# Linear attention and a noisy top-2 mixture of experts: where row buffers lie, which scatters go first, and when the first expert's weights are loaded

## The chip, the cores and the metric

The kernel runs on one core of a Trainium2 chip. The metric is the device time of one execution in microseconds (us). The engines are TensorE (PE; PEld is its weight load), VectorE (DVE), ScalarE (ACT), GpSimd (POOL) and SyncE (SP), which only issues DMAs here.

## The reference

```python
def _attn_ref(q, k, v, lam):                 # q, k, v: 4 x 8 x 768 x 64
    ...
    for b in range(nb):                      # blocks of 64 positions
        intra = np.einsum('bhic,bhjc->bhij', qb, kb) * Dmask[None]
        intra = np.einsum('bhij,bhjd->bhid', intra, vb)
        inter = np.einsum('bhid,bhde->bhie', qb * lam_pow[None], kv_state)
        out[:, :, sl] = intra + inter
        kb_dec = kb * rev_pow[None]
        kv_state = lam_block[None, :, None, None] * kv_state + np.einsum('bhsd,bhse->bhde', kb_dec, vb)
    return out
...
x = attn_out.transpose(0, 2, 1, 3).reshape(B * S, H * D)      # 3072 tokens of 512
...
def _moe_ref(x, w_gate, w_noise, noise, w1, w2):              # 8 experts, 512 -> 1024 -> 512
    noisy_logits = x @ w_gate + np.log1p(np.exp(x @ w_noise)) * noise
    top2 = np.argpartition(-noisy_logits, 2, axis=1)[:, :2]
    ...                                      # softmax over the two chosen logits: top2_w
    for e in range(E):
        for k in range(2):
            mask = top2[:, k] == e
            h = np.maximum(x[mask] @ w1[e], 0.0)
            out[mask] += top2_w[mask, k, None] * (h @ w2[e])
    return out
```

## The kernel before

The order of the instructions on every engine is written out by hand (a manual schedule): each engine runs its instructions in program order, and semaphores are put where data or memory asks for them.

**Attention.** Twelve steps (`for t in range(NST)`, L911) work on two chunks of 128 positions each. A step turns the previous step's output into token rows: `products` and `turn_x` (L424) make transposes on PE, ACT copies them into a row buffer `xc` (two buffers), and `store_x` sends the rows to `x_tok` in DRAM. It transposes keys and queries of the next step (`trans_k`, `trans_q`), updates the state (`kv`), and makes this step's output (`intra`, `inter`, `evac_o`). SP's one queue takes, in program order, the loads of q, k and v three steps ahead, the row stores, the weight loads (`LOADS`) and the zero fill of the output (`zero_out`).

**Expert 0's weights** are loaded in eight pieces of 128 x 1024 floats (512 KB) into `wst` (four buffers, which also hold the one-hot tables `hot` of the routing). Each is split into a high part, a copy on ACT (`HIGH`, `split_high`), and a low part, a subtraction on POOL (`LOW`, `split_low`, L771), in the step that the dictionaries at L61 to L63 name. The last two pieces are split within the expert layers.

**Routing** runs in three groups of eight chunks. `routing(b)` is a generator of small DVE instructions, of which `advance(n)` issues the next n between other work. At its end each group has 16 scatters to send (one for each chunk and choice): indirect DMAs issued by POOL that write records (token, weight) into the list `lst` in DRAM. `scatter(n)` issues the next n; `paced(n, tile)` first puts a small POOL copy of the tile ahead, so that POOL doesn't run ahead of it. `finish(b, False)` issues what is left of a group's DVE instructions.

**From attention to experts.** When the attention pools `ac` and `aw` are closed (L973), the pool `hp` is laid over the same memory, beginning with `ht`, the first layer's output, 128 x 8 x 1664 floats, and then rows of 512 floats: `pv0`, `pv1`, `xg2`, `pv2`, up to `pv6`. An instruction that writes one of the new tiles first waits for everyone who used an old tile under it; for a new tile it waits at its first write, for all old tiles that any part of it covers. Within a pool a name gets its place when it is first used, in the order of first uses, with all its buffers side by side. `xc` is first used at L178 for a constant `hsel`, `kd` in `kdecay(0)` (L337).

Expert 0 takes its tokens in three parts of 2, 2 and 3 tiles of up to 128 tokens (`PARTS0`), gathered from `x_tok` by index (`gather_rows`), transposed and split (`trans_rows`, L818 to L821), through the first layer (`mm1`, L834; `evac1`, L840 on ACT and L844 on DVE) and the second (`gemm2`, L872). Record lists are loaded by SP (`load_rec`). Lists of expert 1 and the gathers of its rows come at L1008 to L1015, in the last part of expert 0: they need all 48 scatters. Then experts 1 to 7 follow in an order by size.

Of the kernel before, what the change touches and what calls it, by code (L numbers as in the profile page):

```python
# [21 lines left out]
FT = mybir.dt.float32  # L22
# [8 lines left out]
B, H, S, D = 4, 8, 768, 64  # L31
C = 128
NC = S // C
NCH = B * NC
HP = H // 2
DM = H * D
DB = DM // 128
# [17 lines left out]
NST = NCH // 2  # L55
# [2 lines left out]
MAXT = 24  # L58
FILLA, FILLB, FILLC = {4: 24, 5: 24, 6: 20, 7: 20, 8: 19, 9: 19, NST - 1: 24}, 2, 4
FILL1, FILL2 = 4, 9  # L60
LOADS = {3: [(1, 0)], 5: [(1, 1)], 6: [(1, 2)], 7: [(1, 3)], 8: [(2, 0)], 9: [(2, 1)], 11: [(2, 2), (2, 3)]}  # L61
HIGH = {5: [(1, 0)], 6: [(1, 1)], 7: [(1, 2)], 8: [(1, 3)], 9: [(2, 0)], 10: [(2, 1)]}
LOW = {6: [(1, 0)], 7: [(1, 1)], 8: [(1, 2)], 9: [(1, 3)], 10: [(2, 0)], 11: [(2, 1)]}  # L63
ZEROS = {10: 8, 11: 8}
MID = 16
X1 = ((), (), (), (), (0, 1), (2, 3, 4), (5, 6))
# [21 lines left out]
def sub(ap, offset, dims):  # L88
    return bass.AP(tensor=ap.tensor, offset=ap.offset + offset, ap=dims)
# [27 lines left out]
def kernel(  # L117
# [3 lines left out]
    nc = tc.nc  # L121
# [9 lines left out]
    aw = att.enter_context(tc.tile_pool(name="aw", bufs=2))  # L131
# [43 lines left out]
    nc.gpsimd.iota(jp, pattern=[[1, 128]], base=0, channel_multiplier=-1)  # L175
    identf = consts.tile([128, 128], FT, name="identf")
    nc.vector.tensor_scalar(identf, jp, 0.0, None, op0=OP.is_equal)
    hsel = aw.tile([128, 2, DB, C], FT, name="xc")[:H, 0].rearrange("h p (s i) -> h p s i", s=2)  # L178
    nc.vector.tensor_copy(hsel, identf[:H, :H].rearrange("h (p s) -> h p s", s=2)[:, :, :, None].to_broadcast([H, HP, 2, 64]))
    pp2 = aw.tile([128, 2 * DB * C], FT, name="xo", bufs=1)[:H, :512].rearrange("p (a i) -> p a i", a=2)  # L180
    pw = pp2[:, 0, :]
# [10 lines left out]
    p = psum.tile([128, H], FT, name="pL")  # L192
# [15 lines left out]
    p = psum.tile([128, HP, C], FT, name="pL")  # L208
# [63 lines left out]
    jobs, scatters, PL = [], [], {}  # L272
    RT = {}

    def advance(n):
        while n > 0 and jobs:
            j = next(jobs[0], "end")
            if j == "end":
                jobs.pop(0)
            elif j == "step":  # L280
                break
            else:
                n -= j or 1

    def finish(b, all_scattered=True):
        while "done" not in RT.get(b, {}):
            advance(1)
        if all_scattered:
            scatter(len(scatters))

    def scatter(n):
        for job in scatters[:n]:
            scatter_list(*job)
        del scatters[:n]
# [117 lines left out]
    def products(u):  # L412

        p = psum.tile([128, 2, C], FT, name="pR")
        for d in range(DB):
            nc.tensor.matmul(p[d * 32:(d + 1) * 32], wgn[:, d, :], XO[u][:, :, d, :], start=True, stop=True)
        XP[u] = aw.tile([128, 2, C], FT, name="xp", bufs=1)
        nc.scalar.activation(XP[u], p, AF.Copy)
# [3 lines left out]
    def turn_x(u):  # L422

        XC[u] = aw.tile([128, 2, DB, C], FT, name="xc")  # L424
        for a in range(2):
            p = bank()
            for d in range(DB):
                nc.tensor.transpose(p[:, d, :], XO[u][:, a, d, :], identf)  # L428
            nc.scalar.activation(XC[u][:, a], p, AF.Copy)
# [188 lines left out]
    def scatter_list(b, c, i):  # L618
        r = RT[b]
        nc.gpsimd.memset(spacer, 0.0)  # L620
        st = nc.gpsimd.indirect_dma_start(  # L621
            out=lst, out_offset=bass.IndirectOffsetOnAxis(ap=r["dest"][:, i, c:c + 1], axis=0),
            in_=r["rec"][:, c, i, :], in_offset=None)
        for s in lst_st:
            tc.declare_no_dep(st.ins, s.ins, reason="every pair of token and choice has its own row")
        for g, s in lst_ld:
            if g < b:
                tc.declare_no_dep(st.ins, s.ins, reason="a later group writes no row of an earlier group's part")
        lst_st.append(st)
# [34 lines left out]
    def paced(n, tile):  # L664
        if scatters:
            nc.gpsimd.tensor_copy(spacer, tile[0:1, 0:1])
            scatter(n)
# [88 lines left out]
    def split_parts(which, e, j, half):  # L756

        st = WS[which, e, j]
        hi, lo = [(W1 if which == 1 else W2)[n][j] for n in range(2)]
        if which == 2:  # L760
            hi, lo = hi.rearrange("p a m -> p (a m)"), lo.rearrange("p a m -> p (a m)")
        r = slice(0, F) if half is None else slice(half * F // 2, (half + 1) * F // 2)
        return st[:, r], hi[:, r], lo[:, r]
# [5 lines left out]
    def split_low(which, e, j, half=None, low=nc.vector):  # L769
        st, hi, lo = split_parts(which, e, j, half)  # L770
        low.tensor_tensor(lo, st, hi.bitcast(FT), op=SUB)  # L771
# [11 lines left out]
    def lists(e):  # L783

        t0 = 0
        for n in PARTS0 if e == 0 else PARTS1:
            full = min(n, NT - 1 - t0)
            yield t0, full, TS
            t0 += full
        if TAILS[e]:  # L790
            yield NT - 1, 1, TAILS[e]

    def load_rec(e, i, queue=nc.sync):

        t0, n, size = list(lists(e))[i]
        nm = f"{i}{size}" if e else f"z{i}"
        r = rp.tile([size, n, RW], I32, name="rec" + nm, bufs=3 if e else 1)
        if e:
            rows = lst[bass.ds(ROW[e] + t0 * TS, n * size), :]
            queue.dma_start(r.rearrange("p n w -> p (n w)"), rows.rearrange("(p n) w -> p (n w)", p=size))  # L800
        else:
            ld = queue.dma_start(r, sub(lst, t0 * TS * RW, [[n * RW, size], [1, n * RW]]))
            if i < NG - 1:
                lst_ld.append((i, ld))
        for j in range(n):
            REC[e, t0 + j] = r[:, j, :]
# [19 lines left out]
    def columns(e, t0, n):  # L826
        return slice(t0 * TS, min((t0 + n) * TS, FULL + TAILS[e]))
# [10 lines left out]
    def evac1(e, t0, n, f, p):  # L838
        cs = columns(e, t0, n)
        nc.scalar.activation(ht(e, 0, f, cs), p, AF.Relu)  # L840
        full = min(cs.stop, FULL) - cs.start
        for r in (slice(0, full), slice(full, cs.stop - cs.start))[:1 + (cs.stop > FULL)]:
            c = slice(cs.start + r.start, cs.start + r.stop)
            nc.vector.scalar_tensor_tensor(ht(e, 1, f, c), p[:, r], 0.0, ht(e, 0, f, c).bitcast(FT), op0=OP.max,  # L844
                                           op1=SUB)

    def ht(e, part, f, c):

        at = c.start + (0 if not part else TAILS[e] if c.start >= FULL else CAP + TAIL)
        return HT[0][:, f, at:at + c.stop - c.start]  # L850
# [60 lines left out]
    for t in range(NST):  # L911
        u = t + 1
        if t:
            products(t - 1)
            turn_x(t - 1)
            paced(1, XC[t - 1][:, 1, 0, :])
        if u < NST:
            trans_k(u)
        load(t + 3, "kt")
        if u < NST:  # L920
            trans_q(u)
        load(t + 3, "qt")
        if u < NST:
            kv(u)
        kdecay(t + 2)
        if u == NST:
            for which, j in LOW.get(t, []):
                split_low(which, 0, j, low=nc.gpsimd)
        scatter(1)
        if u == NST:  # L930
            logits(t - 1)
        intra(t)
        load(t + 3, "vt")
        if t:
            store_x(t - 1)
        inter(t, 0)
        evac_o(t)
        paced(1, XO[t][:, 1, 0, :])
        if t and u < NST:
            logits(t - 1)  # L940
        if 2 * t in GB[1:]:
            if 2 * t > GB[1]:
                finish(GB.index(2 * t) - 2, False)
            jobs.append(routing(GB.index(2 * t) - 1))
        advance(FILLB)
        if u < NST:
            scores(u)
            inter(u, 1)
        for which, j in HIGH.get(t, []):
            split_high(which, 0, j)  # L950
        if u < NST:
            if LOW.get(t):
                nc.gpsimd.tensor_copy(spacer, AT[u][0][0:1, 0, 0, 0, 0:1])
            for which, j in LOW.get(t, []):
                split_low(which, 0, j, low=nc.gpsimd)
        advance(FILLA.get(t, 18))
        for which, j in LOADS.get(t, []):
            load_w(which, 0, j)
        zero_out(ZEROS.get(t, 0))
        if t == 2:  # L960
            turn_noise()
        if t == 4:
            for i in range(4):
                nc.sync.dma_start(sub(lst, i * 128 * LI * RW, [[LI * RW, 128], [1, LI * RW]]), linit)
# [14 lines left out]
        PV.append(hp.tile([128, DM], FT, name=f"pv{t}"))  # L979
    for f in range(2):  # L980
        evac1(0, 0, PARTS0[0], f, head[f])
    finish(1, False)
    for t in range(2, 4):
        gather_rows(0, t, GB[2] * C)
    scatter(sum(job[0] == 0 for job in scatters))
    load_rec(0, 0)
    scatter(1)
    jobs.append(routing(NG - 1))

# [155 lines left out]
    with tc.For_i(0, n_over) as it:  # L1145
# [16 lines left out]
        for f in range(FB):  # L1162
            p = psum.tile([128, OV], FT, name="pS", bufs=4)
# [7 lines left out]
        p = psum.tile([OV, DM], FT, name="pO")  # L1171
# [35 lines left out]
```

## Time and profile before

| | |
|---|---|
| three runs | 754.9, 753.17, 755.08 us; median 754.9 |
| the profiled execution | 752.26 us |
| its span, first to last instruction | 750.4 us |
| PE busy | 722.6 us (96%) |
| PE weight loads busy | 615.5 us (82%) |
| DVE, ACT, POOL busy | 336.6, 238.6, 284.8 us |
| granted clock of PE, mean | 0.991 |

Times in the profile count from the span's start. Idle time in square brackets is that of the engine just before the row, with what ended it, which is inferred from semaphores. SP's and other queues' issues carry a q behind the engine. Matmuls overlap in the pipeline, so the durations of neighbours don't add up. A granted clock of 1.00 is 2.4 GHz.

### The profile page before, as it was taken

The numbers are of one execution on the slowest core, as the hardware profiler recorded it, in microseconds if no ns is written. First come the engines' busy times: TensorE is split into PE (matmuls) and PEld (weight loads), VectorE is DVE, ScalarE is ACT, GpSimd is POOL, SyncE is SP. The second block draws the span as 40 slices with busy tenths as digits, with TensorE's granted clock in tenths as the row PEclk, the third lists the DMA queues.
The fourth block names the chain that finished last, engine by engine and source line by source line (L and its number), as shares of the span: only waits on it lengthen the run. The fifth ranks groups of instructions, "written<-read, shape, count | busy, mean of one in ns | idle before, by whom it ended". The sixth has DMA issues, their size and how long they took to land.

```text
span 750.4 us, 13435 instructions
## 1 busy us (share of the span) xinstructions
PE 722.6 (96%) x5073; PEld 615.5 (82%) x5073; DVE 336.6 (45%) x776; ACT 238.6 (32%) x451; POOL 284.8 (38%) x438
## 2 busy tenths in 40 slices
PE   8899999879988999999999999999999999999996
PEld 6788887669877898898889888988888898889885
DVE  6345978677234444352335243524343343335211
ACT  1666766321123422142214222422132132214200
POOL 3200255558756545423432344234412423220311
PEclk9999999999998999999999999999999999999998
DMA  7999998823517544452434253525352554240210
GB/s 160 219 234 248 217 263 249 258 84 103 138 23 265 171 122 126 142 148 72 151 119 143 71 154 113 145 67 167 113 141 56 164 162 123 61 138 14 78 43 36
DMA packets 112952, 103.20 MB, mean 138 GB/s; under 512 B 85435, under 2 KB 85435, under 8 KB 112885
## 3 DMA queue, kind: packets, MB, share of 16 engines
q1 hardware_dynamic: 98356, 65.94, 34.1%
q0 software_dynamic: 13104, 36.34, 14.9%
q8 instruction: 41, 0.67, 0.4%
q14 instruction: 27, 0.21, 0.1%
q10 hardware_dynamic: 1424, 0.04, 0.1%
HBM read 77.51 MB, written 25.92 MB: 138 GB/s over the span
## 4 chain that ended last, share of the span: by engine, by line
PE 86%; issue 5%; DMA 4%; DVE 2%; POOL 1%; ACT 1%; SPq 1%; ACTq 0%; POOLq 0%
PE pS L834 35%; PE pKV L872 16%; PE pO L872 15%; PE pS L818 3%; PE pS L355 3%; PE pKV L368 2%; PE pO L368 2%; PE pO L877 1%; PE pS L428 1%; PE pS L325 1%; PE pS L312 1%; PE pKV L877 1%; PE pS L400 1%; POOL out_dram L891 1%; DMA wgn<-in_moe_w_noise_dram 1%
## 5 line engine op out<-in xcount | busy, mean ns | idle before, releaser
L834 PE MATMUL pS<-xth,w1h 128*128 128x512 f32 (+3 forms) x544 | 181.7, 334 | 4.1 <-DVE ht L844 3.8
L834 PE MATMUL pS<-xtl,w1h 128*128 128x512 f32 (+3 forms) x544 | 180.5, 332 | 0.8 <-DVE xtl L821 0.8
L834 PE MATMUL pS<-xth,w1l 128*128 128x512 f32 (+3 forms) x544 | 180.4, 332 | 0.0
L844 DVE SCALAR_TENSOR_TENSOR ht<-pS,ht 128x256 fp32r<-128x256 f32 (+3 forms) x176 | 76.6, 455 | 144.3 <-ACT ht L840 142.2
L891 POOL DMA_INDIRECT out_dram<-ot,rec x46 | 65.0, 1412 | 176.1 <-DVE ot L884 165.2
L840 ACT ACTIVATE ht<-pS 128x512 fp32r<-128x512 f32 (+3 forms) x136 | 65.8, 485 | 196.7 <-PE pS L834 187.6
L872 PE MATMUL pKV<-w2h,ht 128*128 128x512 f32 x384 | 125.5, 398 | 0.0
L872 PE MATMUL pO<-w2h,ht 128*128 128x512 f32 x384 | 124.6, 396 | 0.0
L834 PEld LDWEIGHTS pS<-xth,w1h 128*128 128x128 f32 x544 | 102.7, 189 | 13.7 <-DVE ht L844 4.4
L834 PEld LDWEIGHTS pS<-xtl,w1h 128*128 128x128 f32 x544 | 102.7, 189 | 9.6 <-DVE xtl L821 1.0
L834 PEld LDWEIGHTS pS<-xth,w1l 128*128 128x128 f32 x544 | 102.7, 189 | 8.8
L820 ACT ACTIVATE xth<-pS 128x512 fp32r<-128x512 f32 (+2 forms) x53 | 29.6, 572 | 199.6 <-PE pS L818 199.3
L872 PEld LDWEIGHTS pKV<-w2h,ht 128*128 128x128 f32 x384 | 72.8, 190 | 15.5
L872 PEld LDWEIGHTS pO<-w2h,ht 128*128 128x128 f32 x384 | 72.1, 188 | 15.3
L872 PE MATMUL pKV<-w2l,ht 128*128 128x512 f32 x192 | 75.6, 394 | 0.0
L872 PE MATMUL pO<-w2l,ht 128*128 128x512 f32 x192 | 75.2, 391 | 0.0
L856 POOL DMA_INDIRECT pv<-out_dram,rec x46 | 48.9, 1063 | 29.7 <-issue 26.4
L809 POOL DMA_INDIRECT xg<-x_tok,rec x46 | 50.3, 1094 | 21.1 <-issue 14.5
L621 POOL DMA_INDIRECT lst<-recs,dest x48 | 48.7, 1014 | 11.2 <-issue 9.2
L884 DVE SCALAR_TENSOR_TENSOR ot<-pO,rec,pv 128x512 f32<-128x512 f32 x21 | 15.8, 751 | 81.1 <-PE pO L872 81.1
L884 DVE SCALAR_TENSOR_TENSOR ot<-pKV,rec,pv 128x512 f32<-128x512 f32 x21 | 15.8, 751 | 79.8 <-PE pKV L872 79.8
L1123 POOL COPY spacer<-ht 1x1 f32<-1x1 f32 x53 | 9.4, 178 | 105.5 <-ACT ht L840 105.4
(225 smaller groups left out, 953.8 us busy)
## 6 DMA issues: line engine op xcount, KB each, us to landing
wst<-in_moe_w_dram SPq DMA_DIRECT2D x48, 512.0 KB, 4.3
wst<-in_moe_w_dram SPq DMA_DIRECT2D x32, 256.0 KB, 4.1
kt<-in_k_dram SPq DMA_DIRECT2D x24, 256.0 KB, 5.5
qt<-in_q_dram SPq DMA_DIRECT2D x24, 256.0 KB, 5.2
vt<-in_v_dram SPq DMA_DIRECT2D x24, 256.0 KB, 4.9
x_tok<-xc SPq DMA_DIRECT2D x12, 512.0 KB, 4.3
out_dram<-zero SPq DMA_DIRECT2D x3, 2048.0 KB, 12.4
lst<-recs,dest POOLq DMA_INDIRECT x48, 5.0
```

Source lines behind the costliest of these rows:

```text
L355: nc.tensor.matmul(ps[s][:, h, a, :], kT[u][half(s), 2 * r + h, a, :], qT[u][half(s), 2 * r + h, a * C:(a + 1) * C], start=True, stop=True)
L368: nc.tensor.matmul(PO[u][a][half(g), hp, :], lhs, rhs, start=n == 1, stop=n == (8 if u % NW or a else 4))
L621: st = nc.gpsimd.indirect_dma_start(out=lst, out_offset=bass.IndirectOffsetOnAxis(ap=r["dest"][:, i, c:c + 1], axis=0), in_=r["rec"][:, c, ...
L809: nc.gpsimd.indirect_dma_start(out=XG[t][:size(e, t)], out_offset=None, in_=x_tok[:rows, :], in_offset=bass.IndirectOffsetOnAxis(ap=at, ax ...
L820: nc.scalar.activation(hi, p, AF.Copy)
L834: nc.tensor.matmul(p, W1[a][d][:, fs], xt(b, cs)[:, d], start=(d == 0 and i == 0), stop=(d == DB - 1 and i == 2))
L840: nc.scalar.activation(ht(e, 0, f, cs), p, AF.Relu)
L844: nc.vector.scalar_tensor_tensor(ht(e, 1, f, c), p[:, r], 0.0, ht(e, 0, f, c).bitcast(FT), op0=OP.max, op1=SUB)
L856: nc.gpsimd.indirect_dma_start(out=PV[t][:size(e, t), :], out_offset=None, in_=out, in_offset=bass.IndirectOffsetOnAxis(ap=REC[e, t][:, 0: ...
L872: nc.tensor.matmul(p, ht(e, a, f, cs), W2[b][f // 2][:, f % 2, :], start=(i == 0), stop=(i == len(terms) - 1))
L884: nc.vector.scalar_tensor_tensor(o, p, w, pv, op0=MULT, op1=ADD)
L891: st = nc.gpsimd.indirect_dma_start(out=out, out_offset=bass.IndirectOffsetOnAxis(ap=REC[e, t][:, 0:1], axis=0), in_=o, in_offset=None, bo ...
```

## The change

Three edits. The constant `hsel`, which was a view of the first `xc` buffer, becomes a view of the `kd` buffer, so that `kd` gets the place of `xc` in the pool and `xc` one behind all the others. The scatters left over from group 0, and the load of that group's list, are issued ahead of `finish(1, False)` and of the gathers of tiles 2 and 3. Loads of expert 0's weights, and with them the high and low splits, come one step sooner (two loads of the last step are spread over two), so that the last step has no split, and the lines that issued it are dropped.

```diff
-LOADS = {3: [(1, 0)], 5: [(1, 1)], 6: [(1, 2)], 7: [(1, 3)], 8: [(2, 0)], 9: [(2, 1)], 11: [(2, 2), (2, 3)]}
-HIGH = {5: [(1, 0)], 6: [(1, 1)], 7: [(1, 2)], 8: [(1, 3)], 9: [(2, 0)], 10: [(2, 1)]}
-LOW = {6: [(1, 0)], 7: [(1, 1)], 8: [(1, 2)], 9: [(1, 3)], 10: [(2, 0)], 11: [(2, 1)]}
+LOADS = {2: [(1, 0)], 4: [(1, 1)], 5: [(1, 2)], 6: [(1, 3)], 7: [(2, 0)], 8: [(2, 1)], 10: [(2, 2)], 11: [(2, 3)]}
+HIGH = {4: [(1, 0)], 5: [(1, 1)], 6: [(1, 2)], 7: [(1, 3)], 8: [(2, 0)], 9: [(2, 1)]}
+LOW = {5: [(1, 0)], 6: [(1, 1)], 7: [(1, 2)], 8: [(1, 3)], 9: [(2, 0)], 10: [(2, 1)]}
...
-    hsel = aw.tile([128, 2, DB, C], FT, name="xc")[:H, 0].rearrange("h p (s i) -> h p s i", s=2)
+    hsel = aw.tile([128, 2, H, D], FT, name="kd", bufs=1).rearrange("p a h d -> p (a h d)")[:H, :HP * C]
+    hsel = hsel.rearrange("h (p s i) -> h p s i", s=2, i=64)
...
         kdecay(t + 2)
-        if u == NST:
-            for which, j in LOW.get(t, []):
-                split_low(which, 0, j, low=nc.gpsimd)
         scatter(1)
...
+    scatter(sum(job[0] == 0 for job in scatters))
+    load_rec(0, 0)
     finish(1, False)
     for t in range(2, 4):
         gather_rows(0, t, GB[2] * C)
-    scatter(sum(job[0] == 0 for job in scatters))
-    load_rec(0, 0)
     scatter(1)
```

## Rows read from the trace of the kernel before

**Rows 1.** Windows: us, busy us per engine (PE, PEld, DVE, ACT, POOL), clock, DMA share, GB/s.
```profile
100.00:120.00 20.00, 19.26 (x309) 16.61 (x303) 15.07 (x43) 15.06 (x36) 13.04 (x18) 1.00 0.99 229
...
225.00:227.00 2.00, 0.57 (x3) 0.17 (x1) 0.69 (x1) 0.60 (x1) 1.48 (x2) 0.50 1.01 379
...
300.00:400.00 100.00, 100.00 (x529) 85.18 (x528) 41.53 (x74) 26.91 (x44) 37.54 (x46) 1.00 0.41 127
```

**Rows 2.** Waits of PE, whole span: us in total, times, longest us.
```profile
PE pS L818 <- DMA xg<-x_tok,rec: 6.1, 2, 3.7
PE pS L834 <- DVE ht L844: 3.8, 3, 2.1
```

**Rows 3.** Timeline of ACT: start us, us, line, operation, tiles, idle before.
```profile
124.23 1.06 ACT L767 ACTIVATE w2h<-wst 128x1024 fp32r<-128x1024 f32 x1 [4.40 <-DMA wst<-in_moe_w_dram]
...
146.68 1.09 ACT L429 ACTIVATE xc<-pS 128x512 f32<-128x512 f32 x2 [3.25 <-PE pS L428]
153.53 0.66 ACT L840 ACTIVATE ht<-pS 128x256 fp32r<-128x256 f32 x2 [5.76 <-DMA x_tok<-xc]
```

**Rows 4.** Timeline of SP, two of its issues.
```profile
147.79 0.37 SPq L433 DMA_DIRECT2D x_tok<-xc  x1
...
218.47 0.34 SPq L800 DMA_DIRECT2D rec<-lst  x1
```

**Rows 5.** Timeline of DVE, steps 11 and after the attention.
```profile
137.87 2.98 DVE L99 TENSOR_SCALAR wn<-wa 128x8 f32<-128x8 f32 x1
...
153.94 0.76 DVE L844 SCALAR_TENSOR_TENSOR ht<-pS,ht 128x256 fp32r<-128x256 f32 x2 [9.37 <-ACT ht L840]
...
154.81 0.17 DVE L587 CAST idx<-whole 128x2 int32<-128x2 f32 x1
...
169.04 0.23 DVE L497 TENSOR_TENSOR ob<-oh 128x64 bf16<-128x64 f32 x1
...
178.72 0.17 DVE L587 CAST idx<-whole 128x2 int32<-128x2 f32 x1
```

**Rows 6.** Timeline of PE, its waits and the index matmuls.
```profile
126.10 1.15 PE L325 MATMUL pS<-identf,qt 128*128 128x128 f32 x8 [0.85 <-ACT xc L429]
...
148.84 0.41 PE L582 MATMUL pL<-tokab,rest 128*64 128x2 bf16 x8
...
154.42 0.39 PE L834 MATMUL pS<-xth,w1h 128*128 128x256 f32 x1 [2.10 <-DVE ht L844]
...
169.31 0.19 PE L531 MATMUL pL<-ob,lstrict 128*128 128x64 bf16 x1 [1.22 <-DVE ob L497]
```

**Rows 7.** Chain of waits, 169 to 236 us: start us, us, what.
```profile
169.86 0.93 PE pS L818 x8
...
215.28 5.53 PE pO L872 x24
...
222.25 5.69 DMA xg<-x_tok,rec
...
229.09 6.55 PE pKV L872 x24
```

**Rows 8.** Timeline of POOL: subtract, gathers, first and last of scatters.
```profile
138.44 2.36 POOL L771 TENSOR_TENSOR w2l<-wst,w2h 128x1024 fp32r<-128x1024 f32 x1
...
155.75 1.05 POOL L809 DMA_INDIRECT xg<-x_tok,idx  x1 [12.31 <-DVE pp L602]
...
158.43 1.01 POOL L621 DMA_INDIRECT lst<-recs,dest  x1 [0.23 <-issue]
...
162.59 0.96 POOL L621 DMA_INDIRECT lst<-recs,dest  x1 [0.23 <-issue]
...
183.87 1.05 POOL L809 DMA_INDIRECT xg<-x_tok,idx  x1 [0.30 <-DVE wn L99]
...
214.29 0.98 POOL L621 DMA_INDIRECT lst<-recs,dest  x1 [0.16 <-issue]
```

**Rows 9.** Waits of POOL from 156 to 215.27 us.
```profile
POOL lst L621 <- issue: 6.5, 31, 0.6
```

## Prediction

> **What bounds the kernel now.** I read four views in turn. The windows first: from 300 to 400 us TensorE is busy for the whole 100 us, and the expert layers behind it look the same, so nothing that the change touches can shorten them [rows 1]. What can be won lies before 240 us. The waits of PE say where: 6.1 us in two waits for gathered rows, 3.8 us in three waits for the first layer's output [rows 2]. Then the timelines around the end of the attention, and last the chain of waits from 205 to 242 us.
>
> *First stall.* ACT ends its copies of the last pair of row buffers at 146.68 + 1.09 = 147.77, and then does nothing for 5.76 us; what ends that is the store of these rows, issued by SP at 147.79 [rows 3, 4]. Its next instruction is the first copy into ht (L840). That copy reads no row buffer. It waits because ht is laid over the memory of the closed attention pool, xc among it. DVE has nothing to do meanwhile, then starts at 153.94 and works off the routing of groups 1 and 2, up to L497 at 169.04 [rows 5]. PE pays 2.10 us at 154.42, and again 1.22 at 169.31, where it needs L497's result [rows 6].
>
> *Second stall.* PE ends the second layer of tile 4 at 215.28 + 5.53 = 220.81 and then needs two tiles of expert 1's rows. The second of the two gathers goes out at 222.25 and takes 5.69 us [rows 7]. These gathers need the record list, and SP loads it at 218.47, once the last of the 48 scatters (POOL, 214.29) has landed [rows 4, 8]. POOL is what is late there: from 155.75 to 215.27 its waits before a scatter are 31 gaps of issue, the longest 0.6 us, so it simply works [rows 8, 9]. And PE comes out of this stall at half clock: granted 0.50, which is 1.2 of its 2.4 GHz, from 225 to 227 us [rows 1].
>
> **Part 1, xc above ht.** Sizes by the code, in bytes of a partition: ht takes 8 x 1664 x 4 = 53,248. The first 13,792 lie over the pool ac, so 39,456 of aw are covered. aw is laid out by first use, and its tiles are 4,096 each: before kt 2, qt 2, xc 2, xo, at 2, so xc (16,384 to 24,576) is under ht. With hsel in kd the order is kt 2, qt 2, kd, xo, at 2, vt 3, kT, qT, qTs 2, xp, xc 2: xc begins at 62,464. ht then lies over kd, xo, at and part of vt, all read for the last time by the end of turn_x. The seven pv and five xg rows end at 64,032, so only pv6 touches xc, and it is written much later. What is late next: ACT can copy at 147.77; the index (L587) needs PE's L582, which ends at 148.84 + 0.41 = 149.25, so L587 goes from 154.81 to some 149.6, 5.2 earlier, and L497 with it to 164.0 [rows 5, 6]. PE itself, without the three waits of 3.8 us, reaches that point at 169.31 - 1.22 - 3.8 = 164.3 [rows 2, 6]. So **5.1 us** (5.0 to 5.2; no less than 2.1, PE's one wait, and no more than ACT's 5.76).
>
> The move of hsel itself I cost at nothing. Its readers, the QS matmuls, stand on PE right behind the transpose from which the decay factors go out to DRAM and come back before kd is first written. Without that cover, kdecay(0) would wait for eight small matmuls.
>
> **Part 2, scatters first.** POOL sits idle 12.31 us, from 143.44 to 155.75, in front of the gathers of tiles 2 and 3, which wait for that index; the four leftover scatters of group 0 stand behind them and take 158.43 to 163.55, 5.1 us [rows 8]. Ahead of the gathers they fall into the idle time. They wait for nothing new, so no instruction behind them on POOL waits longer. SP's list load then waits only for these. The gathers go at 149.6 + 0.8 = 150.4, and POOL reaches tiles 4 to 6 with 10 us less behind it (5.1 less work, 5.3 earlier start). But those gathers need an index that moves only with PE: 178.72 - 5.1 = 173.6, plus 0.8, so 174.4 in place of 183.87: 9.5 earlier [rows 5, 8]. From there to 214.29 POOL has no wait worth the name [rows 9], and PE, 5.1 earlier, releases each paced scatter in time. The last scatter goes at 204.8, the second gather of expert 1 at 222.25 - 9.5 = 212.8. Before, it landed 5.69 us after its issue, with expert weights loading beside it; so it lands at 218.5 at worst. PE wants it at 220.81 - 5.1 + 0.5 = 216.2: a wait of 0 to 2.3. The weights' loads follow PE's work and not POOL's, so they fall behind the gather now, and I say 0.8, short beside the 3.7 after which the clock fell [rows 2].
>
> What the second stall costs now: from 220.81 to the end of the next second layer, 229.09 + 6.55 = 235.64, is 14.8 us, for two transposes (0.93 in the chain) and 5.53 of matmuls [rows 7]. So 8.4 are lost, half clock included. Taken back: **7.6 us** (6.1 to 8.4).
>
> **Part 3, loads and splits one step sooner.** The subtract that stood in the last step goes to the step before, as all six do. DVE's L99 took 2.98 us there, ending with POOL's 2.36 us subtract; without it the second xtl that the first matmuls need comes earlier by what ACT allows: **0.3 us** (0 to 0.8) [rows 5, 8].
>
> Against this, one 512 KB load more lies ahead of q, k and v from step 4 to 8, on SP's one queue. The 16 engines are busy for 0.99 of 100 to 120 us at 229 GB/s, so it is 2.3 us of transfer [rows 1]. That lateness reaches PE already: ACT waits 4.40 us for a load before its split at 124.23, and PE then waits 0.85 at 126.10 for the row copy behind it on ACT [rows 3, 6]. From below nothing, as the first load goes into a step with slack and HIGH keeps its distance of one step to its load; from above 2.3, paid once, because the queue carries the lag on. I take **1.0 us** lost, between the 0.85 and the 2.3, nearer to the row in which PE pays. Slots of wst turn in the same order one place earlier, and no load meets a slot still in use.
>
> The Trainium skill (DMA: Bandwidth & Descriptors, Issuing engines are not separate DMA queues) says that transfers from SP, ACT and POOL all end on the same 16 engines and interleave, whatever queue issued them. By it the extra load is paid in full, 2.3 us, and the whole would come to 754.9 - 10.7 = 744.2 in place of 742.9, still inside the forecast's own range; the 0.99 agrees, and PE's 0.85 says that part of it is hidden.
>
> **The sum.** 5.1 + 7.6 + 0.3 - 1.0 = 12.0 us. The profiled execution took 752.26 around its span of 750.4 and would take 740.3; the median of the runs, 754.9, lies 2.6 above it. I forecast for the median: 742.9.
>
> **Rivals.** *A: the second stall stays.* Paced scatters stand behind a copy of a tile of PE's making, so POOL may come to the end only as much earlier as PE does. For it: from step to step the pacing is written so. Against: POOL lags PE all the way [rows 9]. It gives 754.9 - 5.1 - 0.3 + 1.0 = 750.5.
>
> *B: the change does not free ht.* If another tile under ht is held until 153.5, only POOL gains: 5.1 us of scatters, so the second gather lands at 227.94 - 5.1 = 222.8 against a need at 221.3, a wait of 1.5: 8.4 - 1.5 = 6.9 back, and 754.9 - 6.9 - 0.3 + 1.0 = 748.7. Against it stands the layout above.
>
> *C: slower, by the loads.* If the queue never carries the lag but each of the six splits holds ACT for its own load, with the next step's xp and xc behind it on ACT and PE behind those, each step pays. It decides from 13.0 / 6 = 2.2 us a step. At 2.6 it is 754.9 - 13.0 + 15.6 = 757.5. For it: 0.99 of the engines, and the 4.40 above. Against: of 4.40 PE paid 0.85. The skill's section above would hold for each load, but it says nothing of paying one load six times.
>
> **Numbers.** The forecast 0.72 (range 740 to 746), A 0.11, B 0.08, C 0.04 at or above 754.9, half of it beyond 0.3%; 0.05 for what I don't see, half of it a gain over 14. 0.3% is 2.3 us and about what a measurement here can tell. Faster 0.93, same 0.04, slower 0.03. The range: below 742.9 less the rest of the second stall (0.8), the loads (1.0) and the 1.7 by which runs of before lie under the median, so 739; above to B and the better half of A, 750.
>
> **What would show it.** ACT's copy into ht right behind the row copies, without an idle time ended by x_tok; four scatters of group 0 between the end of step 11 and the first gather; the list load of expert 1 some 9.5 us earlier and PE's wait for xg under 2.5 us, with no half clock after it; PE's waits before 126 us longer by about 1 us in all. I am wrong if the idle of ACT only changes its name, if POOL shows waits for ht from 187 us on, or if ACT waits over 5 us for its loads in several steps.

## The result, and the profile after

The changed kernel took 743.02 us (median of four runs, 739.96 to 745.84) beside 754.03 us before: a ratio of 0.9855, 95% interval 0.9811 to 0.9898, so 11 us faster (8 to 14). The forecast was 742.9. The profiled execution took 739.96 us around a span of 738.2, so between the two profiles 12.2 us of span are gone, against a sum of 12.0.

Line numbers behind the edits are one higher than before: ht is now written at L841 and L845, the gathers are L810, the scatters L622.

**First stall.** Timeline of ACT in the changed kernel, its last row copies and its first copy into ht:

```profile
147.08 1.08 ACT L430 ACTIVATE xc<-pS 128x512 f32<-128x512 f32 x2 [2.92 <-PE pS L429]
148.05 0.39 ACT L841 ACTIVATE ht<-pS 128x256 fp32r<-128x256 f32 x1
```

Nothing stands in brackets behind the second row: the idle time of 5.76 us that the store of the row buffers ended [rows 3] is gone, and didn't take another name in this profile. The copy comes 5.5 us sooner, though the row copies end 0.4 us later. DVE's routing and PE follow it. First DVE's rows, the index of tiles 2 and 3 and the one-hot of group 1; then PE, which needed the latter:

```profile
149.90 0.17 DVE L588 CAST idx<-whole 128x2 int32<-128x2 f32 x1
...
163.90 0.23 DVE L498 TENSOR_TENSOR ob<-oh 128x64 bf16<-128x64 f32 x1
```

```profile
149.24 0.41 PE L583 MATMUL pL<-tokab,rest 128*64 128x2 bf16 x8
...
164.18 0.19 PE L532 MATMUL pL<-ob,lstrict 128*128 128x64 bf16 x1 [0.20 <-DVE ob L498]
```

The index still comes right behind the matmuls that make it (149.65 to 149.90), which is what limited it in the forecast. PE reaches this place 5.13 us sooner [rows 6], and waits 0.2 us for DVE where it waited 1.22.

**Second stall.** POOL's timeline, leftover scatters of group 0 first:

```profile
143.88 0.95 POOL L622 DMA_INDIRECT lst<-recs,dest  x1 [0.21 <-issue]
...
147.67 0.96 POOL L622 DMA_INDIRECT lst<-recs,dest  x1 [0.21 <-issue]
150.84 1.04 POOL L810 DMA_INDIRECT xg<-x_tok,idx  x1 [2.22 <-issue]
...
174.02 1.04 POOL L810 DMA_INDIRECT xg<-x_tok,idx  x1 [1.63 <-DVE found L593]
...
204.59 0.98 POOL L622 DMA_INDIRECT lst<-recs,dest  x1 [0.16 <-issue]
211.74 1.05 POOL L810 DMA_INDIRECT xg<-x_tok,rec  x1 [6.17 <-DMA rec<-lst]
```

The four scatters fill time in which POOL did nothing for 12.31 us [rows 8]. The gathers of tiles 4 to 6 go 9.85 us sooner, and wait 1.63 us for their index (the last wait named is DVE's L593, right behind PE's index matmuls), so PE paces them now; the last scatter is 9.7 us sooner. SP loads the list, and the chain of waits goes on to PE:

```profile
209.42 0.34 SPq L801 DMA_DIRECT2D rec<-lst  x1
```

```profile
204.59 4.81 DMA lst<-recs,dest
...
209.42 1.55 DMA rec<-lst
...
213.10 3.54 DMA xg<-x_tok,rec
...
216.68 0.66 PE pS L819 x4
217.34 5.51 PE pKV L873 x24
222.85 1.20 PE pS L819 x11
```

The second gather lands after 3.54 us, not 5.69. The second layer that the stall had held ends at 222.85, and ended at 235.64 before [rows 7]: 12.8 us. PE's waits, and the windows (busy us of PE, PEld, DVE, ACT, POOL, then clock, DMA share, GB/s):

```profile
PE pS L326 <- ACT xc L430: 2.3, 2, 1.4
PE pS L819 <- DMA xg<-x_tok,rec: 0.6, 1, 0.6
PE pL L532 <- DVE ob L498: 0.2, 1, 0.2
```

```profile
100.00:120.00 20.00, 18.42 (x277) 15.51 (x276) 13.91 (x40) 15.42 (x36) 12.28 (x18) 1.00 0.86 218
216.00:236.00 20.00, 19.41 (x98) 16.04 (x98) 13.46 (x18) 8.28 (x13) 12.98 (x21) 1.00 0.74 249
300.00:400.00 100.00, 100.00 (x539) 86.03 (x538) 42.60 (x79) 30.30 (x50) 33.47 (x43) 1.00 0.42 124
```

Of 6.1 us of waits for gathered rows 0.6 are left, the wait for ht is no longer in the list, and the clock stays at 1.00 where it fell to 0.50 [rows 1, 2]. What may have been paid for it stands in the first line of each fence: in 100 to 120 us PE is busy for 0.84 us less than before, with the wait for ACT's row copies at its longest, 1.4 us.

### The profile page after: what moved, and what is told of

Its sections match the earlier page's. It is cut to its first block, busy times and chain, and to the rows that moved or that the text cites. A ratio compares the mean times of both kernels' runs of the same rounds, so it can differ in the third digit from the quotient of the medians.

```text
span 738.2 us, 13441 instructions
## 1 busy us (share of the span) xinstructions
PE 717.7 (97%) x5073; PEld 612.1 (83%) x5073; DVE 333.3 (45%) x776; ACT 238.5 (32%) x451; POOL 282.7 (38%) x439
## 4 chain that ended last, share of the span: by engine, by line
PE 82%; issue 5%; DVE 4%; DMA 4%; POOL 1%; ACT 1%; SPq 1%; POOLq 0%; DVEq 0%; ACTq 0%
PE pS L835 34%; PE pKV L873 16%; PE pO L873 14%; PE pS L819 3%; PE pS L356 2%; DMA vt<-in_v_dram 2%; PE pKV L369 2%; PE pO L369 2%; PE pO L878 1%; PE pS L429 1%; PE pS L313 1%; PE pKV L878 1%; PE pS L326 1%; POOL out_dram L892 1%; DVE at L359 1%
## 5 line engine op out<-in xcount | busy, mean ns | idle before, releaser
L845 DVE SCALAR_TENSOR_TENSOR ht<-pS,ht 128x256 fp32r<-128x256 f32 (+3 forms) x176 | 76.6, 454 | 139.1 <-ACT ht L841 137.1
L841 ACT ACTIVATE ht<-pS 128x512 fp32r<-128x512 f32 (+3 forms) x136 | 65.7, 483 | 192.1 <-PE pS L835 188.6
L810 POOL DMA_INDIRECT xg<-x_tok,rec x46 | 50.4, 1096 | 21.6 <-issue 14.5
L622 POOL DMA_INDIRECT lst<-recs,dest x48 | 47.6, 993 | 13.3 <-issue 8.9
```

Source lines behind the costliest of these rows:

```text
L622: st = nc.gpsimd.indirect_dma_start(out=lst, out_offset=bass.IndirectOffsetOnAxis(ap=r["dest"][:, i, c:c + 1], axis=0), in_=r["rec"][:, c, ...
L810: nc.gpsimd.indirect_dma_start(out=XG[t][:size(e, t)], out_offset=None, in_=x_tok[:rows, :], in_offset=bass.IndirectOffsetOnAxis(ap=at, ax ...
```

## Experiments

Ratios are to the kernel before, timed on the same chip beside the kernel in question; brackets hold 95% intervals. Three chips were used, numbers 10, 0 and 4, and before had medians of 757.97, 760.46 and 757.49 on them. It was not profiled there. Its one profile belongs to the first pair, that of the result above, whose chip isn't on record and where its median was 754.03.

The first four kernels ran on chip 10.

**Each part alone, and the first two together.** *layout_only* takes only the `hsel` lines of the change:

```diff
-    hsel = aw.tile([128, 2, DB, C], FT, name="xc")[:H, 0]...
+    hsel = aw.tile([128, 2, H, D], FT, name="kd", bufs=1)...
```

> Theory (two stalls, each with its own cause): the first stall goes, 5 us; the second stays nearly whole, since the four leftover scatters still stand behind the gathers on POOL and POOL starts only some 5 us earlier, as PE does. So 4.5 to 6 us less than before, with a wait of PE for xg of 5 to 7 us and the half clock still there. Rival (the second stall is only the first one passed on): both go, 11 to 13 us less. Rival (the place of xc is without effect): no change, ACT's copy into ht still ended by the store of the rows.

*scatters_only* takes the order of scatters, list load and gathers:

```diff
+    scatter(sum(job[0] == 0 for job in scatters))
+    load_rec(0, 0)
     finish(1, False)
...
-    scatter(sum(job[0] == 0 for job in scatters))
-    load_rec(0, 0)
```

> Theory: the first stall stays (ACT waits some 5.8 us for the store, PE 3.8 us in three waits for ht); POOL gets rid of four scatters in its idle time and ends the list 4.4 to 5 us earlier, so the second stall shrinks to 0.5 to 2.5 us and the half clock goes: 5.5 to 8 us less than before. Rival (paced scatters follow PE): POOL's last scatter stays where it was, no change.

*loads_only* takes the three dictionaries and drops the split of the last step:

```diff
-        if u == NST:
-            for which, j in LOW.get(t, []):
-                split_low(which, 0, j, low=nc.gpsimd)
```

> Theory: about 0.7 us more than before: up to 2.3 us lost where ACT waits for later loads in steps 7 to 9, 0.3 us won at the first xtl; nothing at either stall. Rival (the freed POOL time in the last step is what brings the list forward): 2 us or more less than before.

*without_loads* is the first two diffs together.

> Layout and scatters together, loads as before. Theory: 12 to 13.5 us less than before, which is 0 to 1.5 us less than the changed kernel, because the loads' step costs about 1 us and gives back 0.3. Rival (the loads' step carries part of the gain): 1 us or more slower than the changed kernel.

Measured: layout_only 0.9920 [0.9890, 0.9951], 6 us; scatters_only 0.9856 [0.9820, 0.9892], 11 us; loads_only 1.0015 [0.9985, 1.0045]; without_loads 0.9871 [0.9826, 0.9915], 10 us. The first and the third are as expected in time. In its profile layout_only is not as expected: PE waits 1.4 us for the gathered rows, not 5 to 7, and keeps its full clock there. without_loads came 10 us (6 to 13) faster where 12 to 13.5 were expected. Scatters alone gave more than expected, as much as both together, so the parts don't add up.

**What seemed to be lost in between.** The profile of layout_only has a stall that the profiles of before and of the changed kernel don't have. PE's timeline there, and POOL's:

```profile
161.09 0.40 PE L873 MATMUL pO<-w2l,ht 128*128 128x512 f32 x1 [0.23 <-issue]
...
162.58 0.49 PE L873 MATMUL pO<-w2h,ht 128*128 128x512 f32 x1 [0.86 <-issue]
163.99 0.39 PE L873 MATMUL pO<-w2l,ht 128*128 128x512 f32 x1 [0.93 <-issue]
...
165.41 0.79 PE L873 MATMUL pO<-w2l,ht 128*128 128x512 f32 x1 [0.32 <-issue]
```

```profile
160.49 0.98 POOL L622 DMA_INDIRECT lst<-recs,dest  x1 [0.15 <-issue]
161.96 0.98 POOL L622 DMA_INDIRECT lst<-recs,dest  x1 [0.15 <-issue]
163.43 0.98 POOL L622 DMA_INDIRECT lst<-recs,dest  x1 [0.16 <-issue]
164.89 0.98 POOL L622 DMA_INDIRECT lst<-recs,dest  x1 [0.16 <-issue]
```

PE waits for nothing that the profile names, and moves on some 0.5 to 0.6 us after each scatter's start, for about 5 us; ACT and DVE stand still in the same time (for 6.81 us of ACT's the chain of waits says "another core or an unknown queue"), and the clock is at 0.52 in the mean from 165 to 175 us. The 2 MB zero fill of the output was going out just then (SP issues it at 160.83; in the kernels with scatters first it goes at 151 to 156 us). I took it for the cause, and moved it:

```diff
         if i == 0:
-            zero_out(NTOK // 128)
             advance(50)
...
             for j in range(4):
                 load_w(1, 1, j)
+            zero_out(NTOK // 128)
```

> The kernel before, with only the last 2 MB zero fill of the output issued about 40 us later, behind the loads of the second expert's first weights. If that fill, going out at 160 to 166 us, holds up the engines' instruction fetches, this is 4 to 7 us faster than before and shows no half clock between 160 and 180 us. If the gaps seen there belong to something else, it is within 1.5 us of before.

> The layout part alone, with the same later zero fill. If the fill is what took back part of what the layout gives, 10 to 13 us faster than before, with no gaps of TensorE between 160 and 170 us. If not, 6 to 8 us faster as the layout alone was.

That theory fell. On chip 0, zero_late_before is at 0.9999 [0.9974, 1.0024]; zero_late_layout at 0.9886 [0.9845, 0.9927] is not apart from layout_only. And the stall is still there with no fill beside it, as DVE's timeline in zero_late_before shows:

```profile
169.40 0.17 DVE L488 FIND_INDEX8 mi<-mx,nl 128x8 uint32<-128x8 f32 x1 [0.70 <-issue]
...
170.83 0.17 DVE L488 FIND_INDEX8 mi<-mx,nl 128x8 uint32<-128x8 f32 x1 [0.61 <-issue]
...
172.33 0.18 DVE L491 CAST ei<-mi 128x16 f32<-128x16 uint32 x1 [1.33 <-DVE mi L488]
```

On the same chip the change itself was run again, and the change without its layout part (`hsel` left in `xc`):

> The changed kernel, timed beside the others. If the two stalls are worth their sizes one by one, it is 12 us faster than before. If the parts simply add up as they measured alone (layout 6.9, scatters 11.5, loads a loss of 0.7), it is 17 to 18 us faster. If scatters alone already took what the layout gives, it is 10 to 12 us faster and the run without the layout comes out the same.

> The change with the selector matrix left in the place of the row buffers. The forecast's step (a stall of 5.1 us before the copies of the first layer's output) says 4.5 to 6 us above the changed kernel. The rival, that the row buffers' place costs nothing once the scatters are first, says within 2 us of it.

changed_again: 0.9858 [0.9809, 0.9906], 11 us again, so the parts don't add up to 17. without_layout: 0.9906 [0.9871, 0.9941]. The difference of 0.0048 is 3.6 us, and the medians lie 6.8 us apart; both theories' numbers lie inside the intervals. The two profiles, from one chip, do tell. With `hsel` in `xc`, ACT's wait for the store of the rows is back in front of its first copies into ht (changed_again first, then without_layout):

```profile
149.59 0.66 ACT L841 ACTIVATE ht<-pS 128x256 fp32r<-128x256 f32 x2
153.25 0.66 ACT L840 ACTIVATE ht<-pS 128x256 fp32r<-128x256 f32 x2 [3.49 <-DMA x_tok<-xc]
```

PE reaches the matmul behind the one-hot (L532, here L531) at 165.66 and 169.35. So the layout still works with the scatters first, and is worth 3.7 us at that point, less than the 5.1 forecast.

**Giving the second gain back.** Here POOL alone is made late, after the gathers of tiles 4 to 6, by index fills of a scratch tile that nobody reads (it lies behind ht and moves the row tiles up by 512 bytes). Everything ahead of them stays as in the changed kernel. (*hold_all*: n = 27, *hold_half*: n = 13.)

```diff
                 if f == 3:
                     finish(2, False)
+                    for _ in range(n):
+                        nc.gpsimd.iota(hold, pattern=[[1, 128]], base=0, channel_multiplier=0, ...)
```

> The changed kernel with 27 dummy index fills of 128x128 on GpSimd (about 0.35 us each, 9.5 us in all, the time by which the change brought the last scatter and the list load of expert 1 forward), put among the list scatters at about 182 us, so that everything ahead of it stays as in the changed kernel. If the second stall's gain comes through GpSimd's chain to the gathers of expert 1, the list load goes back to about 219 us, TensorE waits some 8 us for the gathered rows and 7 to 10 us are lost against the changed kernel. If scatters first gains because stalls between 150 and 180 us are gone, under 3 us are lost.

> The same with 13 fills, about 4.6 us. By the chain to the gathers: TensorE's wait for them grows by 3.5 to 4.6 us, of which little is spare now (0.6 to 2.3 us of wait already there), so 3.5 to 6 us are lost against the changed kernel, the upper end if the clock falls as well. By the other theory: under 1.5 us.

The 27 fills took 8.24 us. hold_all is at 0.9969 [0.9939, 0.9999], so 0.0111 above changed_again (each by its own before, as changed_again ran on chip 0 and this on chip 4): 8.4 us given back. With the two half widths (0.0030 and 0.0048, root of the squares 0.0057) that is 4 to 13 us; under 3 us is excluded. Its chain of waits, from the last scatter on, and PE's two waits:

```profile
217.05 4.03 DMA lst<-recs,dest
...
221.10 1.58 DMA rec<-lst
...
224.81 4.36 DMA xg<-x_tok,rec
...
229.22 1.11 PE pS L819 x4
```

```profile
226.94 0.66 PE L819 MATMUL pS<-identf,xg 128*128 128x128 f32 x4 [2.84 <-DMA xg<-x_tok,rec]
229.22 1.11 PE L819 MATMUL pS<-identf,xg 128*128 128x128 f32 x4 [1.62 <-DMA xg<-x_tok,rec]
```

The waits are 4.5 us and not the 8 expected. Beside them stand unnamed gaps of PE, 1.7 us from 214 to 218 us, and the clock, granted 0.79 in the mean from 212 to 236 us. It is at 0.50 already from 218 to 220 us, behind those gaps and ahead of the waits. So not all of the 8.4 us came by the wait for the rows. hold_half (3.93 us of fills) is at 0.9898 [0.9861, 0.9935], 3 us above the changed kernel with an interval that holds zero. Its PE has no wait for gathered rows at all, but unnamed gaps between 208 and 212 us and a clock of 0.66 from 210 to 220, so it says nothing of the chain's slack.

**Scatters alone once more, and loads sooner still.** Both ran on chip 4.

> Scatters first alone, timed in more rounds. By the forecast's terms 7.6 us faster than before; by the run with fewer rounds 11 us (8 to 14). The three kernels with scatters first seen together leave 5 to 12; 7 to 9 would let the parts add up.

scatters_again: 0.9902 [0.9869, 0.9936], 7.4 us. The first time had given 11 us (8 to 14) from five runs; these are six, and the two intervals overlap.

```diff
-LOADS = {2: [(1, 0)], 4: [(1, 1)], 5: [(1, 2)], 6: [(1, 3)], 7: [(2, 0)], 8: [(2, 1)], ...}
+LOADS = {2: [(1, 0)], 3: [(1, 1)], 4: [(1, 2)], 5: [(1, 3)], 6: [(2, 0)], 7: [(2, 1)], ...}
```

> The changed kernel with five weight loads issued one step sooner still, so that they stand two steps ahead of the split that reads them. If ScalarE's waits for those loads (2.6, 4.1 and 5.0 us in the changed kernel) are on the path of TensorE, this is 1 to 2.5 us faster than the changed kernel. If they lie beside other work, it is within 0.7 us of it, or up to 1.5 us slower by the transfers that crowd the earlier steps.

loads_sooner: 0.9848 [0.9811, 0.9884]. Beside 0.9858 of the changed kernel that is no difference, though its profile has none of ACT's waits for these loads left (11.6 us in all in the changed kernel). So they were not a cost that a sooner load gives back, or too small a one to see.

## Why the prediction was right

The median is right to 0.1 us. That is luck in part: the runs of the changed kernel lie between 739.96 and 745.84, and the gain came out at 11.0 us where 12.0 were forecast. In the pair of profiles the gain also came by the mechanisms that were named, point by point:

| step | forecast | measured |
|---|---|---|
| first stall (layout) | 5.1 | 5.5: row copies end 0.4 later, PE's L532 is 5.13 sooner |
| gathers of tiles 2 and 3; of 4 to 6; last scatter | 150.4; 174.4; 204.8 | 150.84; 174.02; 204.59 |
| second gather issued; landed; PE's wait | 212.8; by 218.5; 0.8 | 213.10; 216.64; 0.6 |
| second stall (scatters) | 7.6 | 7.7: 12.8 at the end of that second layer, less 5.13 |
| last step's subtract gone | 0.3 | 0.3: PE 0.73 late at 126 us, row copies 0.4 late at 147 |
| loads sooner | -1.0 | -0.7 at 126 us, in this pair |
| sum | 12.0 | 12.2 of span; 0.6 of the 12.8 is lost again behind 223 us |

*Layout.* That ACT's idle would go and not change its name rested on the order of first uses in the pool. layout_only shows it by its time (6 us, interval 4 to 8), and all profiles agree: ACT waits for the store of the rows before its copies into ht in each of the six without this edit (3.5 to 5.8 us), and in none of the eight with it.

*Scatters first.* In the pair the gain is in the time at which the list of expert 1 can be loaded, as forecast. hold_all shows that the changed kernel has little slack there: POOL alone is made late by about as much, and most of the gain goes.

By which way the edit gains on the other chips is not shown, and by their profiles it isn't the forecast's way. The wait that was to be taken back, 6.1 us for the gathered rows, stands in before's profile alone. In the four others with the old order PE waits 1.2 to 2.3 us for those rows, and has lost its time between 160 and 178 us. In loads_only that is 5.9 us, and then 1.2 for the rows:

```profile
PE pL L531 <- DVE ei L491: 5.9, 1, 5.9
...
PE pS L818 <- DMA xg<-x_tok,rec: 1.2, 2, 0.8
```

layout_only and without_loads, both from chip 10, differ by the order of scatters alone. With the scatters first PE reaches L532 at 166.43 and not at 171.60, so 5.2 us are won there, where the forecast has nothing from this part; the waits for the rows are 1.7 and 1.4 us. So what the edit took away there is a stall that the forecast didn't know, described in the last section, and that about the same time came out is luck. No experiment takes that stall away and keeps the old order.

Rival A (POOL can only be as early as PE lets it) is wrong in the sum, but right about the coupling. In before's profile POOL's paced copies don't wait from 176 us on. In ten of the others, changed_again among them, the last ones wait 1.7 to 2.3 us for ACT's copy into ht, which follows PE. That is one of the forecast's own signs of being wrong; in the profile behind the table it stands with 0.2 us. So in the changed kernel POOL has caught up, and its lag is no longer there to win.

SP's load of the list of expert 1, beside the span, in all profiles:

| kernel | chip | list load of expert 1, us | span, us | difference |
|---|---|---|---|---|
| before | first pair | 218.5 | 750.4 | 531.9 |
| changed | first pair | 209.4 | 738.2 | 528.8 |
| loads_only | 10 | 224.7 | 753.7 | 529.0 |
| layout_only | 10 | 219.7 | 749.1 | 529.4 |
| scatters_only | 10 | 218.7 | 751.8 | 533.1 |
| without_loads | 10 | 213.8 | 745.8 | 532.0 |
| zero_late_before | 0 | 226.4 | 756.7 | 530.3 |
| zero_late_layout | 0 | 218.9 | 749.1 | 530.2 |
| without_layout | 0 | 216.6 | 746.6 | 530.0 |
| changed_again | 0 | 214.3 | 743.3 | 529.0 |
| hold_all | 4 | 221.1 | 752.4 | 531.3 |
| scatters_again | 4 | 218.3 | 746.7 | 528.5 |
| hold_half | 4 | 214.8 | 747.9 | 533.1 |
| loads_sooner | 4 | 214.7 | 744.8 | 530.1 |

The end follows this load by 528.5 to 533.1 us. Most of what the kernels differ by is thus lost or won before it. That doesn't make the load the cause, as anything that holds up PE before it moves both. The 4.6 us of spread are as much as a part is worth: scatters_only loads its list sooner than layout_only and ends later. The profiled run of scatters_only was also the slowest of its five, 753.63 us beside a median of 746.49.

*Loads.* Neither sign nor size is shown. PE's row transposes of that step stand at 126.83, and stood at 126.10 [rows 6], which is 0.73 us in this pair. But in changed_again, the same program, they stand at 125.67 with no wait for the row copies, and over all profiles they lie between 124.2 and 128.8. loads_only is at +1 us (-1 to +3). The Trainium skill (DMA: Bandwidth & Descriptors, Issuing engines are not separate DMA queues) says that DMAs started by SP, ACT or POOL all run on the same 16 engines and interleave. It doesn't say that an added load is paid in full. The 2.3 us that the forecast worked out by it are inside that interval too; the 0.73 of the pair would mean that most of the transfer was hidden.

*The parts by the runs.* If one gives each part one share and fits the eight ratios of kernels made of these parts (each weighted by its interval, the first result included), layout gives 4.4 us, scatters 8.1, loads -1.3, each with a 95% half width of some 3 us, together 11.3. The forecast's shares are 5.1, 7.6 (with 0.3 for the subtract) and -1.0. The runs bear out the sizes no closer than that; the worst misses are the first scatters_only and without_loads, by 0.37 of a percentage point each, in opposite directions. That the parts share nothing is thus compatible with the runs, and not shown.

No version was found that is measurably faster than the changed kernel.

## What to carry to other kernels

When a pool is closed and another laid over it, the first write into the new one can wait for any old tile beneath it, so the tile that is read last belongs where it is written last. Before an engine's queue meets a wait that can't be shortened, look behind it for work that is ready: four scatters moved into a gap of 12 us brought what stands behind them on that engine 5 us forward, and the other 5 came with the index. The time of one event that everything behind it needs, here the list load, tells roughly how much was won ahead of it, on one chip and not closer than the 4.6 us by which it missed here. And profile the old kernel on each chip where parts are timed: here its stall was known from one profile, and on the other chips the time seems to have been lost elsewhere.

## What the runs showed of the hardware that was not expected

Between 160 and 178 us PE, DVE and ACT can stall together, with no releaser that the trace names, and move on in the rhythm of POOL's scatters, every 1.47 us in layout_only. It was in the profiles of layout_only, zero_late_layout, loads_only and zero_late_before, all four with the old order of scatters, on chips 10 and 0, but not in that of before, which was taken in the first pair; with the scatters first, PE's unnamed gaps there are 0.8 us at most. Whether before has it on chips 10, 0 and 4 is not known. Gaps like them, again beside scatters, came at 208 to 218 us in hold_half and hold_all. Moving the 2 MB fill away left the stall. What causes it stays open. Part of what it costs is missing from the wait for the gathered rows later: layout_only waits 1.4 us for them and keeps a clock of 1.00 from 205 to 245 us, where before has 0.91. What it costs in all is not shown.

A stall can be paid in clock as much as in waiting: in hold_all 4.5 us of waits and 1.7 us of unnamed gaps came with a mean of 0.79 over 24 us. By an estimate from its windows of 2 us, PE's busy time times what the clock lacks, that is some 4 us of work at full clock.
